# Retention, Fourier mixing and an MLP on one core: the first batch rebuilt (half tables mirrored, loads and units in another order, sums moved into PSUM)

## The chip, the cores and the metric

The kernel runs on one core of one Trainium2 chip. The metric is the device time of one execution in microseconds (us). Before the change it is 247.04 us, the median of three runs (246.52 to 247.95).

## The reference, cut to what matters

```
# q, k, v: (4, 8, 768, 64) f32;  w_ch1: (512, 2048), w_ch2: (2048, 512) f32
gamma = 1 - 2 ** (-5 - arange(8));  scale = 1 / 8
for t in range(768):                                  # per batch and head
    state = gamma * state + outer(k[t], v[t])
    y[t] = scale * q[t] @ state
x = y as (4, 768, 512)
mixed = real(fft(fft(x, axis=1), axis=2))
u = x + mixed
un = (u - mean(u)) / sqrt(var(u) + 1e-6)              # over the last axis
out = u + relu(un @ w_ch1) @ w_ch2
```

## The kernel before

**Stages of a batch.** The batch has 6 chunks of 128 rows and 4 pairs of heads, worked in the order PAIR_ORDER. For each pair q, k and v are loaded as f32 and cast to f16, k scaled by the decay (`kd`); q and k are transposed on TensorE. `am` multiplies them within a chunk (wkA), `ae` masks and scales the result on VectorE (atm). `kv0` makes one k-v product for each of five chunks (wkK), `sc` (L495) runs the decay over them as a scan. `yi` multiplies atm by v, `yx` multiplies q by the scanned states, both into one PSUM tile (wkY); `x0` (L539) scales that into the rows x. Pairs 0 and 1 of the order fill side 0 of x, pair 2 the columns 2 to 129 of side 1, and pair 3 its columns 130 to 257.

**The Fourier step.** The real part of the two transforms is made from sums and differences. `fold_s` (L679) adds and subtracts the two halves of the rows, `fold_d` (L689) the two sides; `s1` (L736) multiplies by the tables csp and ssp over rows, 193 columns wide, and leaves g; `s2` multiplies g by the tables cd16 and sd16 over columns. Only half of the row frequencies are computed; row blocks 3 to 5 use g mirrored (`gr`, L752). `g0_a`, `g0_b`, `g0_c` make the term of column 0 with the table csn. The tables come from a range reduction in three steps on VectorE (`ts_dve`, `td_dve`; L288, L290, L292) and Abs and Sin on ScalarE (`t_act`, `csn_unit`).

**Row blocks 0 to 2 of batch 0.** `px` (L803) puts half of x's sides into PSUM by multiplying with plus and minus half an identity (hid, nhid), s2 adds the transforms there; ScalarE copies half of the result to qn (L861), VectorE combines it with the other half into u in two instructions (L862, L864). `norm_unit` subtracts the mean (`xmean`, `mean`), giving un; `unT_unit` transposes it.

**The MLP.** For batch 0's first 384 rows `h0_unit(kb, g)` (L953) multiplies one block of 128 rows by four blocks of w1: 16 matmuls. Elsewhere `h_unit` (L936) takes 384 rows. Results are evicted with a relu to ht16, by ScalarE for the rows of ACT_ROWS and by VectorE for the others. `ch_unit` (L979) multiplies by w2, a quarter of a row block per part; L983 makes the output of it, and SP stores it. `rstd_unit` takes the variance (L904, L905) and its root.

**The order.** `first_units` is a list of units for batch 0; each one is pinned behind the one before it on every engine. It ends with un of row block 2; the h0 units stand behind it. Everything else is put out by `emit`, which spreads streams of units over the main line (`majors`: h0, ch, h, ch) by due times between 0 and 1 for each batch (DM0, TS0, DA0, LD0 and so on), and up to time 1.0 `behind` holds it behind the last instruction of `first_units` on its engine; order within an engine is then the tile scheduler's, but POOL's is pinned. All loads of batch 0 are issued by SP at the start, in the order q, k, v of pair 0, of pair 1 and so on. The weights are loaded by POOL (`w1_unit`, `w2_unit`, L993 and L1000). The loads of batch 1 wait for the seventh weight transfer and for `lb[0]["mm"]`, the last matmul of the eighth h0. `filler(n)` multiplies zeros n times (L151); there are 40 such matmuls, all ahead of the first h0.

PSUM has five buffers for general use (`ps_g`), two for y (`ps_y`) and one for the fillers; after `first_units` the last three become `ps_pm`.

Of the kernel before, what the change touches and what calls it, by code (L numbers as in the profile page):

```python
# [18 lines left out]
P = 128  # L19
# [10 lines left out]
PAIR_ORDER = [0, 1, 3, 2]  # L30
ON_ACT = {'q': (0, 1, 0), 'kv': (1, 1, 1), 'g': (0, 1, 1), 'gr': (0, 0, 0)}
FB = 1
DM0, DM1 = (0.120, 0.208, 0.265, 0.344), (0.004, 0.137, 0.232, 0.341)
TS0 = (0.249, 0.368, 0.406, 0.410, 0.479, 0.544, 0.680, 0.685)
TS1 = (-0.040, -0.020, 0.048, 0.585)
DA0, DA1 = (0.068, 0.080, 0.173, 0.203, 0.315, 0.321), (0.063, 0.067, 0.063, 0.158, 0.168, 0.189)
LD0, LD1 = (0.172, 0.226), (-0.370, 0.140)
HT0 = (0.655, 0.675, 0.673, 0.628)
NPE = 2
ACT_ROWS = ((2, 5, 6, 7, 8, 9, 10, 14), (0, 3, 6, 7, 9, 10, 11, 12, 14, 15), (2, 4, 5, 6, 7, 8, 10, 14))  # L40
# [3 lines left out]
def kernel(  # L44
# [13 lines left out]
    def pool(name, bufs, **kw):  # L58
# [37 lines left out]
        "p (n w) -> p n w", n=4)  # L96
    pmask = const.tile([P, 4], f32, tag="pmask")
# [82 lines left out]
    for i in range(4):  # L180
        load_unit(0, i)()
# [3 lines left out]
    icol = const.tile([P, 8], f32, tag="icol")  # L185
# [6 lines left out]
    kf_i = tmp[:, 0, 0:KN].bitcast(i32)  # L192
    kf = tmp[:, 1, 0:KN]
    rs = [tmp[:, 2 + n] if n < 4 else tmp2[:, n - 4] for n in range(10)]
# [6 lines left out]
    nc.gpsimd.iota(kf_i, pattern=[[1, KN]], base=0, channel_multiplier=0)  # L201
    nc.gpsimd.memset(wz, 0.0)  # L202
    filler(6)()
    for h in range(H):
# [3 lines left out]
    nc.vector.tensor_scalar(out=gexp[:, 0], in0=lgrow, scalar1=icol[:, 3:4],  # L208
                            scalar2=float(math.log(0.125)), op0=ALU.mult, op1=ALU.add)
    nc.vector.tensor_scalar(out=gexp[:, 1], in0=lgrow, scalar1=icol[:, 5:6], scalar2=None,  # L210
                            op0=ALU.mult)
    nc.scalar.activation(gexp, gexp, AF.Exp, bias=0.0, scale=1.0)
    for h2 in range(2):
        nc.scalar.activation(gk2[D * h2:D * h2 + D], lgrow[D * h2:D * h2 + D, h2:H:2], AF.Exp,
                             bias=0.0, scale=float(P))
    nc.scalar.activation(icol[:, 6:7], lgrow[:, 0:1], AF.Sin, bias=0.0, scale=1.0)
# [6 lines left out]
    nc.vector.tensor_scalar(out=icoln[:, 0:3], in0=icol[:, 0:3],  # L223
                            scalar1=float(np.float32(1.0 / S)), scalar2=None, op0=ALU.mult)
    nc.vector.tensor_scalar(out=icoln[:, 3:5], in0=icol[:, 3:5], scalar1=float(1.0 / DM),
                            scalar2=None, op0=ALU.mult)
    nc.vector.tensor_copy(kf, kf_i)

    def gk_unit(hp):
        def run():  # L230
            nc.scalar.copy(gk5[:, hp, :, 1:], gk2[:, hp:hp + 1].unsqueeze(1).to_broadcast(
                [P, D, NCH - 2]))
        return run
# [7 lines left out]
    def half_tables():  # L241
        nc.vector.tensor_scalar(out=last[:, 0:1], in0=icol[:, 0:1], scalar1=float(P - 1),
                                scalar2=1.0, op0=ALU.is_equal, op1=ALU.mult)
        for n, (m, a) in enumerate(((-0.5, 1.0), (-1.0, 1.0), (-2.0, 0.0))):
# [8 lines left out]
                                scalar2=1.0, op0=ALU.mult, op1=ALU.mult)  # L253
        nc.vector.tensor_scalar(out=t2[:, 3, 0:128], in0=sd16[:, 0, 1:257:2], scalar1=halve,
                                scalar2=1.0, op0=ALU.mult, op1=ALU.mult)
# [11 lines left out]
    m2 = const.tile([P, 1], f32, tag="m2c")  # L267
    odd = const.tile([P, 1], f32, tag="oddc")

    def parity_consts():  # L270
        nc.vector.tensor_scalar(out=m2, in0=icol[:, 0:1], scalar1=0.5, scalar2=-0.25,
                                op0=ALU.mult, op1=ALU.add)
        nc.vector.tensor_scalar(out=m2, in0=m2, scalar1=MAGIC, scalar2=-MAGIC,
                                op0=ALU.add, op1=ALU.add)
        nc.vector.scalar_tensor_tensor(out=odd, in0=m2, scalar=-2.0, in1=icol[:, 0:1],
                                       op0=ALU.mult, op1=ALU.add)
# [3 lines left out]
        nc.vector.tensor_scalar(out=sgn, in0=odd, scalar1=-2.0, scalar2=1.0,  # L280
                                op0=ALU.mult, op1=ALU.add)

    def trig_dve(idx, n, w, col, coln):
        r = rs[2 * idx][:, 0:w]
        ra = rs[2 * idx + 1][:, 0:w]

# [895 lines left out]
```

## Time and profile before

| | us |
|---|---|
| median of three runs | 247.04 |
| span of the profiled execution | 245.4 |
| first h0 matmul (L953) starts | 35.08 |
| TensorE idle from 35 to 90 us | 0.9 |
| VectorE busy from 25 to 30 us | 4.93 of 5.00 |
| last scan (L495) ends | 26.30 |
| first load of batch 1 is issued | 44.89 |

In the profile PE is TensorE's matmuls, PEld its weight loads, DVE VectorE, ACT ScalarE, POOL GpSimd, SP the queue that issues DMAs. A row of the windows has the window, its length, the busy time of each engine with the number of instructions, the granted clock of TensorE, the share of the DMA engines and GB/s. A row of the order of time has start, duration, engine, line, operation and tiles; in square brackets stands how long the engine was idle before it and what ended that.

### The profile page before, as it was taken

How to read it: one execution, taken by the hardware profiler on the slowest of the kernel's cores; microseconds unless marked ns; L12 is line 12 of the kernel's file. 1: busy time of each engine (PE TensorE's matmuls, PEld its weight loads, DVE VectorE, ACT ScalarE, POOL GpSimd, SP SyncE). 2: the span in 40 equal slices, each digit the busy share in tenths (PEclk: the TensorE clock that was granted, in tenths of full speed). 3: DMA queues.
4: the chain of work that ended last, by engine and by line, in shares of the span. 5: the costliest groups of instructions: out<-in, count | busy, mean ns of one | idle time of the engine just before them, and what ended most of it. 6: DMA issues, size and time to landing. Idle time of an engine off the chain costs nothing.

```text
span 245.4 us, 5309 instructions
## 1 busy us (share of the span) xinstructions
PE 234.2 (95%) x2024; PEld 143.8 (59%) x2024; DVE 177.0 (72%) x430; ACT 124.2 (51%) x276; POOL 81.7 (33%) x146
## 2 busy tenths in 40 slices
PE   6997899999999998999999999999999999999995
PEld 2454668956776655665567546655666455445543
DVE  8997957897897788996885748887895656424112
ACT  8798669587775434751247414742247317202500
POOL 6667601465600057690000646660002405000000
PEclk9999999999999999999999999999999999999999
DMA  8999999699999377999999667786200241221012
GB/s 173 256 260 140 204 195 205 164 245 230 291 229 222 75 168 165 191 181 137 256 272 214 116 141 203 129 120 139 87 1 0 45 151 21 47 85 43 0 45 85
DMA packets 99209, 36.39 MB, mean 148 GB/s; under 512 B 89840, under 2 KB 96240, under 8 KB 99184
## 3 DMA queue, kind: packets, MB, share of 16 engines
q1 hardware_dynamic: 94960, 31.86, 62.2%
q0 software_dynamic: 4224, 4.19, 10.7%
q8 instruction: 16, 0.26, 0.5%
q14 instruction: 9, 0.07, 0.1%
HBM read 27.26 MB, written 6.29 MB: 137 GB/s over the span
## 4 chain that ended last, share of the span: by engine, by line
PE 71%; DMA 7%; DVE 7%; POOL 4%; ACT 4%; SPq 3%; issue 1%; POOLq 0%; ACTq 0%; DVEq 0%
PE psc L979 30%; PE psh L936 25%; DMA k<-in_k_dram 5%; PE ps L736 3%; SPq L165 3%; PE wkA L600 3%; DMA q<-in_q_dram 2%; PE wkY L654 2%; PE pq L833 2%; PE wkY L650 1%; POOL u L870 1%; PE wkK L619 1%; ACT un L885 1%; DVE bst L889 1%; POOL kd L407 1%
## 5 line engine op out<-in xcount | busy, mean ns | idle before, releaser
L979 PE MATMUL psc<-w,ht 128*128 128x512 f16 (+2 forms) x400 | 89.3, 371 | 0.0
L936 PE MATMUL psh<-unT,w 128*128 128x384 f16 x448 | 81.6, 326 | 0.4 <-ACT ht L940 0.2
L979 PEld LDWEIGHTS <-ht 128*128 128x128 f16 x400 | 37.5, 98 | 36.5 <-issue 0.2
L936 PEld LDWEIGHTS <-w 128*128 128x128 f16 x448 | 42.3, 98 | 24.7 <-issue 1.4
L940 ACT ACTIVATE ht<-psh 128x384 f16<-128x384 f32 x64 | 30.9, 489 | 41.7 <-PE psh L936 41.1
L870 POOL TENSOR_TENSOR u<-u,x 128x256 f32<-128x256 f32 x21 | 13.3, 635 | 100.3 <-DVE u L840 91.0
L983 DVE SCALAR_TENSOR_TENSOR ob<-psc,stats,u 128x512 f32<-128x512 f32 (+2 forms) x25 | 18.1, 726 | 26.1 <-PE psc L979 26.0
L942 DVE TENSOR_SCALAR ht<-psh 128x384 f16<-128x384 f32 x48 | 26.2, 548 | 7.7 <-PE psh L936 7.4
L603 DVE TENSOR_TENSOR atm<-wkA,maskp 128x512 f16<-128x512 f32 x36 | 23.8, 681 | 1.6 <-PE wkA L600 1.6
L891 ACT ACTIVATE un<-u,stats 128x512 f16<-128x512 f32 x21 | 15.2, 722 | 16.7 <-DVE stats L890 12.1
L889 DVE BATCH_NORM_STATS2 bst<-u 128x6 f32<-128x512 f32 x21 | 14.6, 694 | 7.7 <-POOL u L872 7.6
L629 DVE SCALAR_TENSOR_TENSOR s<-s,gk,wkK 128x128 f16<-128x128 f16 x48 | 16.3, 341 | 3.7 <-ACT s L625 2.7
L662 ACT ACTIVATE x<-wkY,gexp 128x384 f16<-128x384 f32 x24 | 12.8, 581 | 8.0 <-PE wkY L654 8.0
L151 PE MATMUL wps<-ht 128*128 128x512 f16 x40 | 13.5, 444 | 2.2 <-POOL ht L202 2.2
L383 POOL TENSOR_SCALAR kd<-k,gexp 128x384 f16<-128x384 f32 x24 | 13.8, 585 | 3.6 <-DMA k<-in_k_dram 3.6
L872 POOL TENSOR_TENSOR u<-u,x 128x256 f32<-128x256 f32 x21 | 13.3, 635 | 3.0 <-DVE stats L890 3.0
L600 PE MATMUL wkA<-qTz,kT 128*128 128x256 f16 x72 | 13.4, 273 | 0.1
L835 ACT COPY qn<-pq 128x128 f32<-128x128 f32 x18 | 4.9, 272 | 13.6 <-PE pq L833 13.6
L953 PE MATMUL psh<-unT,w 128*128 128x128 f16 x192 | 11.5, 219 | 0.1
L953 PEld LDWEIGHTS <-w 128*128 128x128 f16 x192 | 11.0, 98 | 0.7 <-issue 0.5
L840 DVE SCALAR_TENSOR_TENSOR u<-pq,g,qn 128x256 f32<-128x256 f32 x18 | 8.5, 472 | 3.3 <-PE psh L936 2.5
L388 POOL TENSOR_SCALAR v<-v 128x768 f16<-128x768 f32 x12 | 10.0, 831 | 1.3 <-DMA v<-in_v_dram 1.3
(164 smaller groups left out, 315.6 us busy)
## 6 DMA issues: line engine op xcount, KB each, us to landing
q<-in_q_dram SPq DMA_DIRECT2D x16, 384.0 KB, 6.3
k<-in_k_dram SPq DMA_DIRECT2D x16, 384.0 KB, 5.6
v<-in_v_dram SPq DMA_DIRECT2D x16, 384.0 KB, 6.3
out_dram<-ob SPq DMA_DIRECT2D x23, 256.0 KB, 2.6
w<-in_moe_w_ch_dram POOLq DMA_DIRECT2D x8, 512.0 KB, 10.8
unT<-un SPq DMA_TRANSPOSE x15, 2.4
out_dram<-ob SPq DMA_DIRECT2D x1, 192.0 KB, 1.9
qTz<-q16z SPq DMA_TRANSPOSE x8, 3.9
```

The lines of the kernel that those rows point to most:

```text
L600: mm = nc.tensor.matmul(wk[:, c2], st["kT"][:, c, :], st["qT"][:, :, c, :], start=True, stop=True)
L603: nc.vector.tensor_tensor(out=st["atm"][:, 2 * part:2 * part + 2], in0=wk, in1=maskp[:, PAIR_ORDER[i]].unsqueeze(1).to_broadcast([P, 2, 2, ...
L629: nc.vector.scalar_tensor_tensor(out=s16[:, c], in0=s16[:, c - 1], scalar=gk2[:, hp:hp + 1], in1=wk[:, c - c0], op0=ALU.mult, op1=ALU.add)
L870: nc.gpsimd.tensor_tensor(out=u[:, kb, 0:256], in0=u[:, kb, 0:256], in1=x[:, kb, 0, 1:257], op=ALU.add)
L889: nc.vector.bn_stats(bst, u[:, kb, :])
L891: una = nc.scalar.activation(un, u[:, kb, :], AF.Identity, bias=stats[:, kb, 0:1], scale=-1.0)
L936: nc.tensor.matmul(psh, w116[:, cb, fb * P:(fb + 1) * P], unT[:, cb, rt * 384:(rt + 1) * 384], start=(cb == 0), stop=(cb == 3))
L940: nc.scalar.activation(ht16[:, fb, :], psh, AF.Relu, bias=0.0, scale=-1.0)
L942: nc.vector.tensor_scalar(out=ht16[:, fb, :], in0=psh, scalar1=-1.0, scalar2=0.0, op0=ALU.mult, op1=ALU.max)
L953: mm = nc.tensor.matmul(psh[:, f], w116[:, cb, fb * P:(fb + 1) * P], unT[:, cb, kb * P:(kb + 1) * P], start=(cb == 0), stop=(cb == 3))
L979: nc.tensor.matmul(psc[:, c0:c1], ht16[:, fb, rb3 * P:(rb3 + 1) * P], w216[:, fb, c0:c1], start=(fb == 0), stop=(fb == NFB - 1))
L983: nc.vector.scalar_tensor_tensor(out=ob[:, c0:c1], in0=psc[:, c0:c1], scalar=lb[b]["st"][:, rb, 3:4], in1=lb[b]["u"][:, rb, c0:c1], op0=AL ...
```

## The change

- Batch 0's twelve loads are issued in the order LOADS: q0, k0, q1, k1, v0, q2, v1, k2, q3, k3, v2, v3.
- The range reduction covers 194 and 129 columns instead of 386 and 257. Its steps are single units on a named engine (`trig`). The other halves of the tables are mirrored by `mir_s` and `mir_d` with a sign per partition; csn is copied out of csp. `turn_d` makes tables for the upper columns with the sign turned.
- Casts, copies and evictions of batch 0 take the engine as an argument ("A" ScalarE, "V" VectorE, "P" GpSimd).
- The second half of the columns no longer goes through fold_d. Its S1 product is summed in PSUM from both sides: the part of side 0 early (`s1a_pre`, `s1b_pre`), that of side 1 after the last fold_s (`s1a_fin`, `s1b_fin`). `minus_unit` supplies side 0 with its sign turned.
- Row blocks 0 to 2: px puts x itself into PSUM with the identity, and `s2e_unit` adds both halves of the columns there, eight matmuls per row block instead of four. `un0_unit` takes un straight out of PSUM; u is written later by `u0_unit`. qn, mu and the two combining instructions go away. Row block 0 is split in two PSUM tiles.
- The list `first_units` is in a new order and holds the h0 units, `g0`, csn and `u0` too; in `majors` twelve empty units stand in their place. The PSUM pools are exchanged in the list (`second`).
- The fillers: six at the start and six single ones, 12 in place of 40.
- The due times and ACT_ROWS have other values; the sine half of the tables t2 has its sign turned.

```diff
+LOADS = (('q', 0), ('k', 0), ('q', 1), ('k', 1), ('v', 0), ('q', 2), ('v', 1), ('k', 2), ('q', 3), ('k', 3), ('v', 2), ('v', 3))
+SW, DW = 194, 129
-DM0, DM1 = (0.120, 0.208, 0.265, 0.344), (0.004, 0.137, 0.232, 0.341)
-TS0 = (0.249, 0.368, 0.406, 0.410, 0.479, 0.544, 0.680, 0.685)
+DM0, DM1 = (0.225, 0.285, 0.339, 0.379), (0.019, 0.164, 0.328, 0.362)
+TS0 = (0.237, 0.364, 0.355, 0.47, 0.519, 0.549, 0.621, 0.693)
...
-LD0, LD1 = (0.172, 0.226), (-0.370, 0.140)
+LD0, LD1 = (0.262, 0.373), (-0.339, -0.001)
...
-ACT_ROWS = ((2, 5, 6, 7, 8, 9, 10, 14), (0, 3, 6, 7, 9, 10, 11, 12, 14, 15), (2, 4, 5, 6, 7, 8, 10, 14))
+ACT_ROWS = ((2, 4, 5, 6, 7, 8, 9, 10, 11, 13), (0, 1, 4, 5, 7, 8, 9, 10, 14, 15), (1, 4, 5, 8, 9, 10, 12, 13, 14, 15))
...
-    for i in range(4):
-        load_unit(0, i)()
+    for name, i in LOADS:
+        load0(name, i)
...
+    def trig(idx, part, eng):
+        n, w, c = (S, SW, idx) if idx < 3 else (DM, DW, idx)
+        r, ra = rs[2 * idx][:, 0:w], rs[2 * idx + 1][:, 0:w]
+
+        def run():
+            if part == 0 and eng == "A":
+                nc.scalar.activation(ra, kf[:, 0:w], AF.Copy, bias=MAGIC, scale=icoln[:, c:c + 1])
+            elif part == 0:
+                eng_of(eng).tensor_scalar(out=ra, in0=kf[:, 0:w], scalar1=icoln[:, c:c + 1],
+                                          scalar2=MAGIC, op0=ALU.mult, op1=ALU.add)
+            elif part == 1:
+                eng_of(eng).tensor_scalar(out=ra, in0=ra, scalar1=-MAGIC, scalar2=float(n),
+                                          op0=ALU.add, op1=ALU.mult)
+            else:
+                eng_of(eng).scalar_tensor_tensor(out=r, in0=kf[:, 0:w], scalar=icol[:, c:c + 1],
+                                                 in1=ra, op0=ALU.mult, op1=ALU.subtract)
+        return run
...
+    def mir_s(which, eng):
+        def run():
+            tab = (csp, ssp)[which]
+            dst = bass.AP(tensor=tab.tensor, offset=tab[:, 0, 0, 97:98].offset,
+                          ap=[list(tab.ap[0]), [3 * NK - 1, 2], [NK, 3], [1, 96]])
+            src = bass.AP(tensor=tab.tensor, offset=tab[:, 0, 0, 95:96].offset,
+                          ap=[list(tab.ap[0]), [3 * NK, 2], [NK, 3], [-1, 96]])
+            scaled(eng, dst, src, (sgn, nsgn)[which])
+        return run
...
+    def minus_unit(eng):
+        def run():
+            dst, src = fd[0]["eo"][:, 1, :, :, 128:256], fd[0]["ab"][:, :, :, 0, 130:258]
...
+    def s1_last(part, e, c0, c1, start, pars=(0, 1)):
+        ps, off = (fd[0]["psA"][:, e], 0) if c1 == 64 else (fd[0]["psB", e], c0)
...
+        for par in pars:
+            for sb in range(3):
...
+                nc.tensor.matmul(ps[:, par, c0 - off:c1 - off], lhs, tab[:, par, sb, c0:c1],
+                                 start=start and par == 0 and sb == 0, stop=False,
+                                 skip_group_check=True)
...
+            for n, (dst, rhs) in enumerate(((lo[:, 0:256], x[:, 0, 1:257]),
+                                            (lo[:, 256:257], x[:, 1, 257:258]),
+                                            (up, x[:, 1, 256:1:-1]))):
+                nc.tensor.matmul(dst, ident16, rhs, start=n == 0 or n == 2 and kb in SPLIT,
+                                 stop=False, skip_group_check=True)
...
+    def s2e_unit(kb, cb, halves=(0, 1)):
+        def run():
+            g = fd[0]["g"]
+            for half in halves:
+                for e in range(2):
+                    tab = ((cd16, sd16), (cdr, sdr))[half][e]
+                    nc.tensor.matmul(lb[0]["pq", kb, half], g[:, 2 * e + cb, kb * P:kb * P + P],
+                                     tab[:, cb], start=False, stop=cb == 1 and e == 1,
+                                     skip_group_check=True)
+        return run
...
+            if eng == "A":
+                una = nc.scalar.activation(un, pq, AF.Identity, bias=xm, scale=-1.0)
+            else:
+                una = nc.vector.tensor_scalar(out=un, in0=pq, scalar1=-1.0, scalar2=xm,
+                                              op0=ALU.mult, op1=ALU.add)
...
+            trig(3, 1, "V"), q0_unit(2), ae_unit(0, 1, 0), gk_unit(1), filler(1), kv0_unit(1),
+            ae_unit(1, 0, 1), trig(3, 2, "V"), x_edges(1), t_act(4, 0), ae_unit(0, 0, 0),
+            ae_unit(1, 1, 0), sc_unit(1), t_act(3, 2), yi_unit(0, 0), k0_unit(2, 0, "A"),
...
+            am_unit(3, 1), ae_unit(3, 0, 1), t_act(1, 2), t_act(4, 1), sc_unit(2), t_act(0, 2),
+            v0_unit(3, 0, 3, "A"), yx_unit(2), x0_unit(2, 0, "A"), s1a_pre(0), yi_unit(2, 1),
+            x0_unit(2, 1, "A"), w1_unit(1), ae_unit(3, 0, 0), v0_unit(3, 3, 6, "P"), kv0_unit(3),
+            ae_unit(3, 1, 0), t_act(3, 1), ae_unit(3, 1, 1), yi_unit(3, 1), s1b_pre(0),
+            turn_d(1, "P"), mir_s(1, "A"), yi_unit(3, 0), sc_unit(3), w1_unit(2), w1_unit(3),
+            yx_unit(3), s1b_pre(1), s1a_pre(1), fold_s(0, 0, 130, 1, 2, (0,), "V"),
+            fold_s(0, 0, 130, 1, 2, (1,), "V"), fold_d(0, 0, (0,), "V"), s1_mm(0), parity_b,
+            x0_unit(3, 0, "A"), fold_d(0, 0, (1,), "V"), s1_mm(1), x0_unit(3, 1, "A"),
+            fold_s(0, 130, 258, 1, 2, (0,), "V"), s1a_fin(0),
+            fold_s(0, 130, 258, 1, 2, (1,), "V"), s1b_fin(0), s1a_fin(1), g_unit(0, "V"),
+            mir_d(0, "A"), turn_d(0, "P"), g_unit(1, "A"), s1b_fin(1), px_unit(0),
+            s2e_unit(0, 0, (0,)), ga_unit("V"), xmean_unit(0), gb_unit(0, "V"), gr_unit(1, "V"),
+            s2e_unit(0, 1, (0,)), s2e_unit(0, 0, (1,)), s2e_unit(0, 1, (1,)), gb_unit(1, "V"),
+            px_unit(1), un0_unit(0, 0, "A"), unT0(0, 0), ut0(0, 0, "A"), w2_unit(0),
+            xmean_unit(1), s2e_unit(1, 0, (1,)), s2e_unit(1, 1, (1,)), un0_unit(0, 1, "V"),
+            unT0(0, 1), s2e_unit(1, 0, (0,)), second, s2e_unit(1, 1, (0,)), ut0(0, 1, "V"),
+            h0_unit(0, 0), px_unit(2), s2e_unit(2, 0, (1,)), un0_unit(1, 2, "V"), unT0(1, 2),
...
+            h0_unit(2, 0), csn_unit(0, "V"), h0_unit(2, 2), csn_unit(1, "P"), g0_unit(0, (1,)),
+            g0_unit(0, (2,)), u0_unit(0, 0, "V"), u0_unit(2, 2, "V"), u0_unit(0, 1, "A"),
+            u0_unit(1, 2, "A"),
+        ]
...
         if b == 0:
-            for kb in range(3):
-                if kb:
-                    majors.append(unT_unit(0, kb))
-                majors += [h0_unit(kb, g) for g in range(4)]
+            majors += [lambda: None] * 12
```

## The prediction

> **What bounds the kernel now.** I read the span and the busy shares first, then the busy time by windows, then the order of time up to 50 us, last the waits of TensorE.
>
> ```profile
> span 245.4 us, 5309 instructions
> ...
> PE 234.2 (95%) x2024; PEld 143.8 (59%) x2024; DVE 177.0 (72%) x430; ACT 124.2 (51%) x276; POOL 81.7 (33%) x146
> ```
>
> The page: the span of the profiled execution is 245.4 us, the median of the runs 247.04 us, so 1.6 us lie around the span and are added at the end. The windows show where PE is not full (time, then PE, PEld, DVE, ACT, POOL busy):
>
> ```profile
> 10.00:15.00 5.00, 4.66 (x74) 2.83 (x69) 4.61 (x14) 4.40 (x10) 3.30 (x6) 1.00 1.27 250
> ...
> 25.00:30.00 5.00, 4.29 (x57) 2.75 (x53) 4.93 (x13) 3.39 (x8) 3.37 (x5) 1.00 1.23 203
> 30.00:35.00 5.00, 4.70 (x39) 3.17 (x39) 3.99 (x12) 2.96 (x11) 0.00 (x0) 1.00 1.24 206
> 35.00:40.00 5.00, 4.85 (x75) 4.22 (x74) 2.77 (x10) 4.39 (x16) 0.26 (x4) 1.00 1.18 193
> ...
> 90.00:245.00 155.00, 151.24 (x1108) 88.57 (x1105) 101.69 (x235) 59.87 (x141) 43.23 (x73) 1.00 0.56 117
> ```
>
> From 35 us on PE is full: idle 0.9 us up to 90 us, and 3.8 us after that, of which 2.9 us are the last eviction and store. Ahead of 35 us part of PE's busy time is the 40 fillers (L151), and DVE is the fullest engine with work (4.93 of 5.00 us). So the kernel is a **start of 35 us, set by loads and DVE, and then a queue of PE work**. A change to the first batch is worth: how much earlier the first h0 matmul (L953) starts, minus PE work that it puts behind that point. The order of time shows the start (start, us, engine, line):
>
> ```profile
> 7.70 0.98 POOL L423 TENSOR_SCALAR v<-v 128x768 f16<-128x768 f32 x1 [0.38 <-DMA v<-in_v_dram]
> ...
> 15.34 0.59 POOL L407 TENSOR_SCALAR kd<-k,gexp 128x384 f16<-128x384 f32 x1 [0.82 <-DMA k<-in_k_dram]
> ...
> 17.04 0.94 POOL L423 TENSOR_SCALAR v<-v 128x768 f16<-128x768 f32 x1 [0.55 <-DMA v<-in_v_dram]
> ...
> 25.49 0.81 DVE L495 TENSOR_TENSOR_SCAN s<-gk,wkK 128x320 f16<-128x320 f32 x1
> ...
> 28.74 0.62 DVE L679 TENSOR_TENSOR xab<-x 128x384 f16<-128x384 f16 x2
> 29.39 1.03 DVE L689 TENSOR_TENSOR eo<-xab 128x768 f16<-128x768 f16 x2
> ...
> 35.08 3.00 PE L953 MATMUL psh<-unT,w 128*128 128x128 f16 x48
> ```
>
> A cast that waits for a DMA tells when it lands. Three loads take 4.65 us (v at 7.70, 12.37, 17.04); a q lands 1.2 us after the load before it, a k or v 1.7 to 1.8. The last scan ends at 26.30, the last fold_s at 29.36, h0 starts at 35.08.
>
> **The change, part by part.**
>
> Loads. The same twelve in a new order; by these spacings k3 lands at 18.2 (before: cast at 21.41), v0 at 10.7 (before 7.70), v2 at 19.9, v3 at 21.6 as before. SP issues nothing else until 44.89. The chain behind v is cast, kv0, scan, yx; the chain behind k has transposes, am, ae and yi too, so what lands last has less behind it.
>
> Tables. The trig steps on DVE cost 1.3 + 1.9 + 2.0 us (386 wide: L288, L290, L292) and 0.7 + 1.1 + 2.0 us (257 wide): 9.0 us. Halved in width and with six of fifteen steps on ACT and POOL some 2.5 us stay on DVE. ACT's table functions (L316 to L325, L301: about 10 us) go to some 5 us, and mirroring adds about 2.5 us on ACT and POOL. DVE takes in exchange three of eight te copies (no row; L925, 512 f16 out of PSUM on DVE, is 0.40 us, so 0.6; above that the 0.80 of ACT's L447), one x0 (nearest L942, 0.55) and one half of k0.
>
> DVE then has this to do between the scan of the first pair and the last fold_s: 4 scans at 0.81 (3.2), 14 ae at 0.49 (6.8; L471, 7.9 us for 16), two te (1.2), x0 (0.5), two trig steps of 129 (0.4 to 0.6), fold_s 1.00 + 0.63 + 0.62, fold_d of the first half 1.03, parity_b 0.35, and one wait of 0.3 for yi of pair 1: 16.1 us. The first scan can't start until v0 has landed, 10.7, been cast on POOL, 0.9, and kv0 has run, 0.5: **12.2 us**. So the last fold_s ends at 28.3, against 29.36. The bounds: if te takes 0.80, the trig steps 0.8 us more and ACT (by the same count full to 24 us) is late with x0, 29.4, no gain; if DVE were free, the chain behind v3 alone counts: 21.6 + cast 0.55 + kv 0.47 + scan 0.81 + yx 0.46 + two x0 1.05 + fold_s 0.62 = 25.6. I take 28.3, for DVE has no hole in that stretch for the order to fill.
>
> From the last fold_s to h0. Before: second fold_d, S1, copies, s2, two evictions, un, transposes, copies: 35.08 - 29.36 = 5.7 us. After: fold_d and the qn and u steps leave this path. PE has left: 18 short S1 matmuls at 0.065 (between L953's 0.0625 and L736's 0.087): 1.2; px twice 0.5; twelve s2e matmuls at 0.11 (L849: two in 0.22) 1.8 with their changes of weights, less what overlaps; two half transposes 0.25: 3.8 us with hand-overs of 0.1. Beside it run ga and gb on DVE (0.35 each), g_unit on ACT (0.60), un0 (0.40) and ut0 (0.37): none is later than the PE step that wants it, by 0.3 us for the tightest (un0 of the first half at 30.95, its transpose 31.0). If that cover is gone, each adds its own 0.4. Start of h0: 28.3 + 3.9 = **32.2 us, 2.9 earlier**. Bounds: 29.5 to 35.
>
> PE work put behind that point: px(2) 0.25, eight s2e of row block 2 0.9 (its four s2 matmuls stood ahead of h0 before), g0_b 0.37 (nine at 0.04, before in an idle spot): **+1.5 us**. The 28 fillers less free no time by themselves: they stood in PE's idle time.
>
> Weights. w1(0) is issued on POOL near 19.6 instead of 20.41, w2 near 29 to 31.5 instead of 25.4 to 28.4, both still ahead of the DMA engines (share 1.2 from 25 to 40 us). The loads of batch 1 (before at 44.89) wait for the eighth h0 and w_dma[6], both some 2.5 us earlier: no cost taken; up to 1.5 us if the weights slip.
>
> Behind h0. Retuned due times and ten ACT rows instead of eight, ten and eight: PE's idle time there, about 2 us without the end, is all that can be won; taken as 0, bounds -1.5 and +4 (below).
>
> Sum: -2.9 + 1.5 = -1.4 us on 245.4: 244.0, and with the 1.6 us around it **245.6 us**.
>
> **Rivals.**
>
> *The start shrinks to what the v chain needs* (the order found is better than my count): last fold_s at 25.6 to 26.5, h0 at 29.5 to 30.4: -4.7 to -5.6 + 1.5: 243 to 244. For it: v3 is the only landing after 20 us. Against: DVE's 16 us.
>
> *Debt behind h0: slower.* In the trace the s2 of row blocks 3 to 5, the zeroing of qTz and the eight maskp (ACT, 1.7 us) run under h0, from 38 to 50 us. Now all of batch 0's h0 belong to the pinned list, and behind() keeps everything else behind its last instruction on each engine, at 46.5 us. DVE then has u0 0.95, zeros 1.5, three bn 2.6 (L904, L905), three s2 with bn 5.5 (0.96 + 0.87 each), three ob evictions 2.2: 12.8 us, to 59.5 us; POOL casts batch 1 only behind the u adds, at 56 (before 49.19). PE has s2 1.3 and twelve ch parts 10.3 until 58.1, then needs unT of row block 5, which comes at 59.5 or later, or the casts. Up to 1.4 us of stall some first transposes of batch 1 fill; from 2.6 us on it is slower by over 0.5%. With 4 us: 248.2; and later casts could carry it to 249.
>
> *PE loses its full rate: slower.*
>
> ```profile
> 2.15 2.74 PE L151 MATMUL wps<-ht 128*128 128x512 f16 x6 [2.15 <-POOL ht L202]
> ...
> 7.89 0.81 PE L151 MATMUL wps<-ht 128*128 128x512 f16 x3
> ```
>
> The first six fillers take 0.46 us each, those at 7.89 take 0.27, though the granted clock reads 1.00 in both windows: PE ran at half rate until it had been busy for some 5.5 us. With 12 fillers instead of 40 PE is busy about half the time from 8 to 28 us. If it falls back, the 3.8 us to h0 grow by about 2.5 and the first h0 by up to 1.7: 248 to 250. Against: no PE hole of my count is longer than 1.5 us. The Trainium skill (TensorE: Matmul & The Clock Gate, "Part 1: The HAM clock gate") gives a window of 3.4 us of idleness for the fall and as much activity for the rise; by that rule the rate would hold here, and the trace's rise after 5.5 us is of that order.
>
> *It changes nothing*: new waits between queues that are worked in order eat the 2.9 us: 246.5 to 247.5.
>
> **How the numbers follow.** 0.5% (1.2 us) is about what a measurement of this kernel can tell from no change. Chances: my sum 0.48 (its own range 244.4 to 246.8, two thirds of it below 245.8), v chain 0.23, debt 0.14, half rate 0.08, nothing 0.07. Faster: 0.32 + 0.23 = 0.55. Slower: 0.12 of the debt's, 0.08: 0.20. Same: the rest, 0.25. Low end: between the v chain's times, less 1 us for idle time won behind h0, 242.3; high end 249.0, in the half rate's span.
>
> **What would show it.** First L953 matmul near 32.2; last scan near 25.7 with DVE over 95% busy from 12 to 28 us; v3's cast at 21.7 or later and not the last wait; no PE hole over 0.5 us between 28 and 46; h0 done near 46, s2 of block 3 only after that. Wrong if DVE has holes ahead of the scans (then loads or POOL casts set the start), if 128-column matmuls take 0.1 us after 28 us, or if PE idles over 1 us between 55 and 62.

## The result and the profile after

The changed kernel takes **251.27 us** (median of 4 runs, 251.03 to 251.92) against 247.02 us (4 runs, 246.52 to 247.95): a ratio of 1.0174, 95% interval 1.0150 to 1.0198. It is slower by 4.3 us, where 1.4 us faster was forecast, and it lies above the forecast's high end of 249.0. In the changed kernel the lines are: L155 filler, L483 transposes, L492 te, L509 am, L516 ae, L531 kv0, L540 scan, L559 yi, L571 yx, L724 fold_s, L947 s2e, L1126 h0. In runs that add a line to the kernel they are one higher (L541 scan, L1127 h0).

The page of the kernel after: the span, the engines, and the granted clock in 40 slices.

```profile
span 249.0 us, 5322 instructions
...
PE 234.2 (94%) x2041; PEld 146.8 (59%) x2041; DVE 174.2 (70%) x415; ACT 123.7 (50%) x278; POOL 81.0 (33%) x148
...
PEclk9759799999999999999999999999999999999999
```

PE's busy time is the same 234.2 us as before, in a span that is 3.6 us longer. Ahead of h0 it is 28.9 us before and 26.8 after, with 28 fillers fewer; behind h0 it is 2.2 us more. The clock row, full before, has holes in the first 30 us. The windows of the kernel after:

```profile
10.00:15.00 5.00, 3.91 (x42) 2.39 (x41) 4.05 (x11) 4.35 (x11) 2.71 (x5) 0.50 1.25 257
15.00:20.00 5.00, 4.58 (x60) 3.16 (x59) 4.28 (x8) 2.88 (x6) 2.32 (x6) 0.59 1.30 243
20.00:25.00 5.00, 3.39 (x59) 2.09 (x57) 4.77 (x9) 3.46 (x7) 4.26 (x7) 1.00 0.43 60
25.00:30.00 5.00, 4.43 (x76) 3.64 (x74) 4.29 (x11) 3.82 (x11) 1.88 (x3) 0.66 1.14 181
...
60.00:65.00 5.00, 3.77 (x41) 2.71 (x41) 4.42 (x15) 4.91 (x8) 5.00 (x8) 1.00 1.12 262
65.00:80.00 15.00, 14.48 (x184) 10.33 (x182) 13.56 (x36) 12.50 (x26) 4.53 (x7) 1.00 0.91 188
```

DVE is not full between 10 and 30 us (4.05 to 4.77 of 5.00), the DMA engines fall to a share of 0.43 from 20 to 25 us, and behind h0 PE has a hole of 1.23 us at 60 to 65 and 0.52 at 65 to 80. The order of time on DVE, ahead of h0, shows the waits (start, duration, then in brackets the idle time and what ended it):

```profile
13.03 0.82 DVE L540 TENSOR_TENSOR_SCAN s<-gk,wkK 128x320 f16<-128x320 f32 x1 [0.91 <-PE wkK L531]
...
18.36 0.96 DVE L492 COPY qTz<-tq 128x768 f16<-128x768 f16 x1 [0.37 <-PE tq L483]
...
22.15 0.95 DVE L492 COPY qTz<-tq 128x768 f16<-128x768 f16 x1
23.02 1.31 DVE L724 TENSOR_TENSOR xab<-x 128x774 f16<-128x774 f16 x2
...
28.04 0.82 DVE L540 TENSOR_TENSOR_SCAN s<-gk,wkK 128x320 f16<-128x320 f32 x1 [0.68 <-PE wkK L531]
...
30.98 0.63 DVE L724 TENSOR_TENSOR xab<-x 128x384 f16<-128x384 f16 x2 [0.39 <-ACT x L337]
```

The last fold_s ends at 31.61, not 28.3, and the row of all h0 matmuls puts the first at 35.1, where it was before:

```profile
L1126 PE MATMUL psh<-unT,w x192: 218/219/219, 35.1 to 47.3; 128*128 128x128 f16 x192
```

POOL's order of time shows two things: `mir_s(0)` holds up the queue for 2.8 us until ACT has made csp, with POOL's half of k3's cast and w1's first transfer behind it; and behind h0 the u adds begin at 53.73 (42.44 before), so that the casts of batch 1 begin at 58.59 (49.19 before).

```profile
20.66 0.75 POOL L339 TENSOR_SCALAR csp<-csp,sgn 128x576 f16<-128x576 f16 x1 [2.81 <-ACT csp L325]
21.38 0.58 POOL L453 TENSOR_SCALAR kd<-k,gexp 128x384 f16<-128x384 f32 x1
21.91 0.96 POOL L1167 DMA_DIRECT2D w<-in_moe_w_ch_dram  x1
...
53.73 0.64 POOL L1055 TENSOR_TENSOR u<-u,x 128x256 f32<-128x256 f32 x1 [17.70 <-DVE stats L1081]
...
58.59 0.83 POOL L415 TENSOR_SCALAR q16z<-q 128x768 f16<-128x768 f32 x1
```

The account of the two profiled executions, then: start of h0 35.1 in both; from there to the end 210.3 us before and 213.9 after. PE's busy time in that stretch is 205.3 us in 1699 matmuls before and 207.5 in 1721 after (+2.2), its idle time 5.0 and 6.4 (+1.4).

### The profile page after: what moved, and what is told of

The parts are those of the page before. It is cut to its first block, busy times and chain, and to the rows that moved or that the text cites. A ratio compares the mean times of both kernels' runs of the same rounds, so it can differ in the third digit from the quotient of the medians.

```text
span 249.0 us, 5322 instructions
## 1 busy us (share of the span) xinstructions
PE 234.2 (94%) x2041; PEld 146.8 (59%) x2041; DVE 174.2 (70%) x415; ACT 123.7 (50%) x278; POOL 81.0 (33%) x148
## 4 chain that ended last, share of the span: by engine, by line
PE 74%; DVE 7%; DMA 6%; ACT 5%; POOL 4%; SPq 2%; issue 2%; ACTq 0%; DVEq 0%
PE psc L1153 29%; PE psh L1109 22%; PE psh L1126 4%; DMA unT<-un 3%; PE ps L856 2%; PE wkA L645 2%; DMA k<-in_k_dram 2%; DVE atm L516 2%; PE wkY L699 2%; PE wkY L695 1%; DMA v<-in_v_dram 1%; ACT kT L612 1%; POOL u L1057 1%; PE pq L1027 1%; ACT un L1070 1%
## 5 line engine op out<-in xcount | busy, mean ns | idle before, releaser
L1153 PE MATMUL psc<-w,ht 128*128 128x512 f16 (+2 forms) x400 | 88.3, 370 | 0.0
L1113 ACT ACTIVATE ht<-psh 128x384 f16<-128x384 f32 x70 | 34.0, 490 | 46.9 <-PE psh L1109 46.5
L1115 DVE TENSOR_SCALAR ht<-psh 128x384 f16<-128x384 f32 x42 | 22.9, 551 | 9.9 <-PE psh L1109 9.5
L1070 ACT ACTIVATE un<-u,stats 128x512 f16<-128x512 f32 x21 | 15.2, 722 | 15.8 <-DVE stats L1069 10.6
L1126 PE MATMUL psh<-unT,w 128*128 128x128 f16 x192 | 11.4, 219 | 0.0
L1126 PEld LDWEIGHTS <-w 128*128 128x128 f16 x192 | 11.0, 98 | 0.1
L645 PEld LDWEIGHTS <-kT 128*128 128x128 f16 x72 | 6.8, 98 | 4.6
L724 DVE TENSOR_TENSOR xab<-x 128x780 f16<-128x780 f16 (+4 forms) x18 | 8.8, 526 | 0.8 <-ACT x L337 0.4
```

The costliest lines, as they stand in the source:

```text
L645: mm = nc.tensor.matmul(wk[:, c2], st["kT"][:, c, :], st["qT"][:, :, c, :], start=True, stop=True)
L1070: nc.scalar.activation(un, u[:, kb, :], AF.Identity, bias=stats[:, kb, 0:1], scale=-1.0)
L1113: nc.scalar.activation(ht16[:, fb, :], psh, AF.Relu, bias=0.0, scale=-1.0)
L1115: nc.vector.tensor_scalar(out=ht16[:, fb, :], in0=psh, scalar1=-1.0, scalar2=0.0, op0=ALU.mult, op1=ALU.max)
L1126: mm = nc.tensor.matmul(psh[:, f], w116[:, cb, fb * P:(fb + 1) * P], unT[:, cb, kb * P:(kb + 1) * P], start=(cb == 0), stop=(cb == 3))
L1153: nc.tensor.matmul(psc[:, c0:c1], ht16[:, fb, rb3 * P:(rb3 + 1) * P], w216[:, fb, c0:c1], start=(fb == 0), stop=(fb == NFB - 1))
```

## The experiments

"H0" is the start of the first h0 matmul, "scan to h0" the time from the start of the first scan to it. The first scan lies between 12.5 and 13.4 us in kernels whose lists agree up to there, so H0 carries some scatter that scan to h0 leaves out. In five profiles whose list up to h0 is that of the kernel after, H0 is 34.9 to 35.4, and in a sixth, d1_s2e, 36.2: one profile each doesn't carry a difference of some tenths. Times are medians of 4 runs (f3_late 10, h4_mend 6); ratios are to the kernel before, run beside each, whose median lay between 246.5 and 247.2. Differences in time below are taken from the ratios. The intervals of e1_warm, e2_pool, e4_fence, e9_norm and d1_s2e overlap that of the kernel after, so their times alone don't tell them from it.

| run | edit | time | ratio, 95% | H0 | scan to h0 |
|---|---|---|---|---|---|
| before | | 247.02 | 1 | 35.1 | 23.3 |
| after | | 251.27 | 1.0150-1.0198 | 35.1 | 22.1 |
| f1_few | before, 12 fillers | 249.36 | 1.0075-1.0131 | 37.3 | 25.6 |
| e1_warm | after, 40 fillers | 250.41 | 1.0110-1.0166 | 34.0 | 21.1 |
| e2_pool | after, mir_s(0) late | 250.78 | 1.0133-1.0189 | 34.4 | 21.3 |
| d2_te | after, te copies cut | 249.72 | 1.0086-1.0132 | 34.0 | 20.9 |
| e3_te | after, te on ACT | 254.12 | 1.0244-1.0318 | 36.8 | 24.0 |
| l1_loads | after, old loads | 252.43 | 1.0197-1.0241 | 36.8 | 22.6 |
| h1_three | e1, e2, d2 | 249.33 | 1.0056-1.0122 | 34.1 | 20.7 |
| d1_s2e | after, s2e doubled | 252.52 | 1.0188-1.0248 | 36.2 | 23.1 |
| e4_fence | after, early fence | 250.53 | 1.0133-1.0176 | 34.9 | 22.2 |
| e5_due | after, old due times | 253.05 | 1.0226-1.0286 | 34.9 | 22.1 |
| e6_rows | after, old ACT rows | 253.76 | 1.0252-1.0298 | 35.4 | 22.8 |
| e9_norm | after, sums under h0 | 250.96 | 1.0139-1.0221 | 35.0 | 22.1 |
| h2_best | e1, e2, e9 | 249.56 | 1.0059-1.0115 | 33.5 | 21.0 |
| h4_mend | h2 and more | 251.46 | 1.0153-1.0213 | 36.5 | 23.1 |
| f2_rows | before, new ACT rows | 249.74 | 1.0080-1.0114 | 34.8 | 23.1 |
| f3_late | before, new later batches | 247.77 | 1.0007-1.0036 | 35.1 | 23.3 |

### The start

**Fillers.** e1_warm puts 28 fillers into nine lines of the new list, so that it has 40, as many as the kernel before; its recorded expectation counts 22 and 34. f1_few takes 28 out of the old list, the same number that the change takes out. One line of each edit, e1_warm's first:

```diff
-            filler(1), icoln_unit, te_unit(0, 1, "V"), am_unit(0, 0), trig(3, 0, "A"),
+            filler(3), icoln_unit, te_unit(0, 1, "V"), am_unit(0, 0), filler(6), trig(3, 0, "A"),
...
-              q0_unit(0), t0_unit(0, 0), filler(4), ts_dve(1), te_unit(0, 0), t_act(0, 2),
+              q0_unit(0), t0_unit(0, 0), filler(1), ts_dve(1), te_unit(0, 0), t_act(0, 2),
```

> The changed kernel with 22 more filler matmuls in the gaps of the first batch (34 of the 40 of before). Theory clock: TensorE at half rate from 9 to 20 us and from 27 to 30 us is what ate the 2.9 us expected of the start; at full rate its steps there are shorter, the first h0 matmul moves from 35.09 to 33 to 34, the time falls by 1 to 2 us. Rival theory, queues: VectorE's list and waits on casts set the start, the rate hardly matters; h0 at 34.7 to 35.5, time within 0.5 us. In both the granted clock reads 1.00 from 10 us on.

> The kernel before with 12 filler matmuls instead of 40, nothing else. Theory clock: without them TensorE falls to half rate here too, somewhere between 8 and 30 us; h0 starts at 35.6 to 36.6 instead of 35.08 and the time is up 0.5 to 1.5 us. Rival (the old order keeps TensorE busy enough, or its rate does not matter where VectorE is full): rate 1.00 or h0 within 0.3 us, time within 0.4 us; fillers out of the way could even win 0.3.

With 40 fillers PE keeps its rate (the clock reads 1.00, and six wkY matmuls take 0.35 us and the ten of kv0 0.47 all along) and H0 comes 1.1 us earlier. The time falls by 0.9 us. In the old list the cut alone costs 2.5 us. The same six S1 matmuls in f1_few, and in the kernel before, in the order of time on PE:

```profile
28.70 1.15 PE L736 MATMUL ps<-csp,eo 128*128 128x193 f16 x6 [0.55 <-DVE eo L689]
```

```profile
28.41 0.69 PE L736 MATMUL ps<-csp,eo 128*128 128x193 f16 x6 [0.41 <-DVE eo L689]
```

They take 1.15 instead of 0.69 us: PE has lost its full rate on the very path to h0, with no hole longer than 1.25 us on PE ahead of it. In f1_few the last fold_s ends at 29.65 (29.36 before) and h0 begins 7.7 us later instead of 5.7, so nearly all of its loss lies in that chain.

**One instruction in POOL's queue.** e2_pool moves mir_s(0) behind v3's cast.

```diff
-            mir_s(0, "P"), ae_unit(2, 1, 1), filler(1), te_unit(3, 0, "V"),
+            ae_unit(2, 1, 1), filler(1), te_unit(3, 0, "V"),
...
-... v0_unit(3, 3, 6, "P"), kv0_unit(3),
+... v0_unit(3, 3, 6, "P"), mir_s(0, "P"), kv0_unit(3),
```

> The changed kernel with mir_s(0) moved on GpSimd from ahead of k0(3) to behind the cast of v3; it stood 2.8 us waiting for ScalarE's table and held up k0(3), the issue of w1(0) and the cast of v2. Theory queues (head of the line): k0(3) at 18.5 to 19.5 instead of 21.38, w1(0) issued by 20.2 instead of 21.91, loads of batch 1 at 43.5 to 44.5 instead of 45.63, h0 0.3 to 1 us earlier, time down 0.3 to 1 us. Theory VectorE's work alone: weights and loads earlier as said, h0 within 0.2 us, time within 0.3 us.

w1's first transfer is issued at 18.95 instead of 21.91, POOL's half of k3 is cast at 18.42 instead of 21.38, the DMA share from 20 to 25 us is 1.09 instead of 0.43, and H0 comes 0.7 us earlier. That the edit did this is not shown. Up to the third scan nothing on DVE moved, and the gain lies behind it, where PE in this execution kept its rate. DVE in the kernel after, then DVE and the window of 25 to 30 us in e2_pool:

```profile
25.18 0.80 DVE L540 TENSOR_TENSOR_SCAN s<-gk,wkK 128x320 f16<-128x320 f32 x1
```

```profile
25.20 0.80 DVE L540 TENSOR_TENSOR_SCAN s<-gk,wkK 128x320 f16<-128x320 f32 x1
...
27.48 0.82 DVE L540 TENSOR_TENSOR_SCAN s<-gk,wkK 128x320 f16<-128x320 f32 x1
```

```profile
25.00:30.00 5.00, 4.31 (x89) 3.48 (x88) 4.86 (x12) 4.61 (x13) 2.90 (x4) 1.00 0.61 87
```

The last scan waits for nothing here; in the kernel after it waited 0.68 us for a kv0 of 0.74 us, which takes 0.47 in e2_pool. PE does the same work at the same times up to 26.5 us in both, and then the same kind of six psA matmuls takes 0.50 us in the one and 0.35 in the other. Whether the edit or chance kept the rate, one profile can't tell, and the times don't differ.

**VectorE's share of the copies.** d2_te leaves most of the q copies of te out of VectorE; e3_te gives them back to ScalarE.

```diff
-                    "p (t c) -> p t c", c=NCH), tq.rearrange("p c t -> p t c"))
+                    "p (t c) -> p t c", c=NCH)[:, 0:n], tq.rearrange("p c t -> p t c")[:, 0:n])
...
-            te_unit(2, 0, "V"), t_act(1, 0), q0_unit(3), mir_d(1, "P"), t_act(1, 1),
+            te_unit(2, 0, "A"), t_act(1, 0), q0_unit(3), mir_d(1, "P"), t_act(1, 1),
```

> The changed kernel, but the copies of the q table that stand on VectorE take only 16 of the 128 columns of each chunk, so part of the mixed-in table is left out. It takes 0.95 us to some 0.2 from each of the two copies in DVE's list ahead of the last fold. The theory that DVE's list is full there: the last fold_s ends 1.0 to 1.5 us earlier (31.6 in the changed kernel) and h0 starts at 33.6 to 34.1 (35.1). The rival, that waits for ScalarE's and PE's products set the scans and DVE's work fits into them: less than 0.4 us of it arrives at h0, and the time stays within 0.5 us.

> The changed kernel with the two strided q copies te(2,0) and te(3,0), 0.96 and 0.95 us on VectorE, given back to ScalarE. Theory VectorE's work: its list from the first scan to the last fold_s is 1.9 us shorter, last fold_s ends near 30 instead of 31.6, h0 at 33.3 to 33.8, time down 1.2 to 1.8 us. Theory queues (waits for other engines set the start, ScalarE is as full): h0 at 34.5 to 35.5, time within 0.6 us.

d2_te: 1.4 us less on DVE, H0 1.1 us earlier, 1.6 us faster: the list counts. e3_te, which moves te(3, 0) as well, missed: scan to h0 grew by 1.9 us, with 4.6 us of waits in ae and the scans. But in its profile PE stood at half rate until about 31 us, so that six wkY matmuls took 0.50 us as late as 29.84:

```profile
29.84 0.50 PE L559 MATMUL wkY<-v,atm 128*128 128x64 f16 x6
```

The same half rate goes with 1.0 us more from scan to h0 in d1_s2e below. So about half of the loss can be ScalarE's, and this run doesn't divide it. All four runs of e3_te (252.75 to 254.79 us) are slower than those of the kernel after, so ScalarE was no better place for the copies.

**Loads.**

> The changed kernel with the loads of the kernel before in their order: q, k and v of one pair together, where the change puts the four v behind. By my sum v2 and v3 last free the k and q tables of the last pairs 1.7 to 1.9 us earlier, at the price of v0 coming later: k3's cast moves from 21.4 to about 23, the last scan from 28.0 to 29.5 or later, and h0 from 35.1 to 36 to 37. The rival, that the last scan waits for compute and not for a load: h0 within 0.5 us of 35.1, and then the new order of loads brought nothing.

`LOADS` as before, q, k, v by pairs: H0 36.8, 1.7 us later, and 1.1 us slower. Of the 1.7 us, 1.2 stand at the first scan already (14.21 instead of 13.03), where the order of loads was to act; the rest comes in an execution whose clock stayed low for longer (0.72 from 30 to 35 us instead of 1.00).

**All three at once.**

> The changed kernel with three things at once: 22 more fillers, mir_s(0) behind v3's cast on GpSimd, and the two q table copies of VectorE's list cut to 16 of 128 columns (part of the mixed-in table is left out). One by one they brought h0 forward by 1.06, 0.74 and 1.09 us from 35.09. If they are separate causes (rate, waits, VectorE's work) they add up: last fold_s near 28.7, h0 at 32.0 to 32.6, which is where my forecast put it, and a time 2.5 to 3 us under the changed kernel's, 248.3 to 248.8. The rival is one common limit that each of them eased: h0 not before 33.4 and a time over 249.3.

They don't add up: H0 34.1, scan to h0 shorter by 1.4 us, not by the 3.0 of the three runs together. Divided at the third scan:

| run | first to third scan | third scan to h0 |
|---|---|---|
| after | 12.15 | 9.91 |
| e1_warm | 11.29 | 9.82 |
| e2_pool | 12.05 | 9.15 |
| d2_te | 11.01 | 9.89 |
| h1_three | 10.90 | 9.83 |

e1_warm and d2_te gain ahead of the third scan, and their gains overlap there; e2_pool's gain, behind it, is gone in h1_three. DVE's order of time in h1_three:

```profile
24.26 0.82 DVE L541 TENSOR_TENSOR_SCAN s<-gk,wkK 128x320 f16<-128x320 f32 x1 [0.60 <-PE wkK L532]
...
27.21 0.82 DVE L541 TENSOR_TENSOR_SCAN s<-gk,wkK 128x320 f16<-128x320 f32 x1 [0.76 <-PE wkK L532]
```

The scans wait for kv0, and kv0 stands on PE behind a transposition's copy on ScalarE (0.89 us of wait in am) and behind three fillers (0.8 us each time). With less work DVE only waits more, for PE, ACT and DVE hand each pair round. PE and DVE are some 85% busy between the first scan and the last fold_s here, and ACT 76%.

### Behind h0

**The work put there.** d1_s2e issues the eight s2e matmuls of row block 2 twice; all eight units stand behind the first h0 in the list, not six of them as its expectation says.

> The changed kernel with the eight s2e matmuls of row block 2 (six of the eight stand behind the start of h0, all of them in PE's full stretch) issued twice, so that row block 2 gets its transform twice. My forecast put 0.9 us on them as part of 1.5 us of PE work that h0's move leaves behind its start, counted in full. If that is right, the time grows by 0.8 to 1.0 us, to 252.1 to 252.3, and h0 stays at 35.1 within 0.5. The rival, that the work behind h0 hides in PE's later waits (1.8 us of them between 50 and 80 us): less than 0.4 us.

The time grows by 1.1 us, its interval touches that of the kernel after (1.0188 against 1.0198), and H0 moved too, by 1.1, in a list that is the same up to h0. The order of time of its PE shows why (first row), beside that of the kernel after (second):

```profile
19.88 0.50 PE L559 MATMUL wkY<-v,atm 128*128 128x64 f16 x6 [0.42 <-DVE atm L516]
```

```profile
19.84 0.35 PE L559 MATMUL wkY<-v,atm 128*128 128x64 f16 x6 [0.42 <-DVE atm L516]
```

In this execution PE stood at half rate until 31.4 us, though its clock column reads 1.00. From h0 to the end it has 0.5 us more than the kernel after, PE busy 0.7 more. So the work put behind h0 costs between nothing and about its own time; one for one is not shown.

**The cover.** e4_fence lets everything else start behind the exchange of the PSUM pools instead of behind the whole list; e9_norm puts the sums, the three s2 and their norms among the h0 units. e7_under and e8_all did the same without moving the norms back: DVE's bn then stood in its queue waiting for POOL's u, h0 itself waited 2.5 and 3.4 us for an eviction, and the times were 253.98 and 254.17; they say nothing of the debt.

```diff
-    base.update(tails)
+        if u is second:
+            base.update(tails)
...
+            u0_unit(2, 2, "V"), h0_unit(0, 1), unT0(2, 2), ut0(2, 2, "A"), s2_unit(0, 3),
+            h0_unit(1, 3), s2_unit(0, 4), h0_unit(1, 1), norm_unit(0, 3), h0_unit(0, 3),
+            s2_unit(0, 5), norm_unit(0, 4), h0_unit(2, 3), unT_unit(0, 3), h0_unit(2, 1),
+            h0_unit(2, 0), unT_unit(0, 4), h0_unit(2, 2), norm_unit(0, 5),
```

> The changed kernel with the fence (the instructions that hold everything else behind the first batch) taken ahead of the first h0 instead of behind the last unit. By the instruction order the zeroing of qTz, the half tables and maskp then run under h0; s2 of row blocks 3 to 5 still comes behind h0. Theory debt: 1.5 us of zeros and 1.7 us of maskp less ahead of s2; u adds at 52 instead of 53.73, casts of batch 1 at 56.5 to 57 instead of 58.59, TensorE idle from 55 to 80 us 0.3 to 1.0 instead of 1.75, time down 0.5 to 1.3 us. Rival (the PSUM tiles held until u0, or the loads, set it): idle and time within 0.4 us.

> The changed kernel with h0's cover used for the rest of batch 0: its sums csn, g0, gr and u0, the last three s2 chunks and the norms of mix 0 stand among the h0 units instead of behind them, and each norm stands two h0 units behind its s2, so that DVE isn't held at a bn that waits for POOL's u. The debt theory (VectorE and GpSimd come out of h0 some 9 us behind, and PE pays for it between 50 and 80 us): the batch-1 casts start at 48.5 to 50 (58.6 in the changed kernel), PE's idle from 50 to 80 is under 0.5 us, and the time is 1.2 to 2 us under the changed kernel's, 249.3 to 250. The rival (the idle behind h0 is a matter of the order of ScalarE's and PE's lists, not of the debt): the idle from 50 to 80 stays above 1.2 us and the time within 0.5 us of the changed kernel's. An h0 that itself waits for DVE (an ht eviction over 1 us late) would make it no test.

e4_fence: u adds at 51.50, casts at 56.35; 0.5 us faster by the ratios, within their intervals, of which H0 explains 0.2. PE's waits moved from 60 to 50-60 us, and from 55 to 80 us it is idle for 1.5 us where 0.3 to 1.0 was expected. e9_norm paid the debt, casts at 49.62, and won nothing (250.96). Its POOL, and its PE, by the order of time:

```profile
49.62 0.83 POOL L415 TENSOR_SCALAR q16z<-q 128x768 f16<-128x768 f32 x1 [0.18 <-PE psh L1127]
```

```profile
47.41 0.40 PE L1097 MATMUL pst<-ident,un 128*128 128x128 f16 x4 [1.10 <-ACT un L1071]
...
50.20 0.40 PE L1097 MATMUL pst<-ident,un 128*128 128x128 f16 x4 [0.61 <-ACT un L1071]
```

The idle time from 50 to 80 us fell from 1.77 to 0.82, and 1.51 us appeared between 45 and 50, where PE waits for un in the two rows above. We read this as the chain s2, u, bn, un, transpose waited for at another place; its length was not measured.

**Due times and rows.**

> The changed kernel with the due times DM0, TS0 and LD0 of before; the fence behind the last unit of the first batch stays. Theory debt: what starves TensorE from 60 to 65 us (1.2 us idle) is that GpSimd's u adds and then the casts of batch 1 come late, because the variance of row blocks 0 to 2 stands ahead of s2 on VectorE; with s2 first the u adds start near 51.5 instead of 53.73, the casts near 56 instead of 58.59, the idle time from 60 to 80 us falls from 1.7 to under 0.6 us, time down 0.8 to 1.7 us. Rival, late loads: the loads of batch 1 (45.63) set it; idle time and time within 0.4 us.

> The changed kernel with the rows of the table that ScalarE evicts in the later batches as they were before. They act only behind batch 0, so h0 stays at 35.1 within 0.3. My forecast put nothing on them: the time within 0.5 us of the changed kernel's. The rival, that the new split is part of the 3.6 us by which the stretch behind h0 is longer: 1 us or more faster, with PE's idle from 90 us on under 4 us (4.68 in the changed kernel, 3.76 before).

> The kernel before with the change's ten ACT rows in each place instead of eight, ten and eight, and nothing else. In the changed kernel the old rows cost 2.5 us. If the new rows are better by themselves (VectorE relieved where it holds up PE), the kernel before gets 0.5 to 2.5 us faster, and then the first batch of the change costs more than the whole change shows. The rival, that the rows only fit the new due times: 247.0 or slower.

> The kernel before with the change's ACT rows and its due times for the later batches (the second values of DM, DA and LD, and TS1); batch 0 is the old one throughout. If the later batches of the change are better by themselves, it is 0.5 to 3 us faster than the kernel before and PE's idle from 90 us on falls below 3.3 us (3.76). The rival, that these values are neutral and fitted to the new first batch: within 0.6 us of 247.0, or slower.

Each old value in the new kernel costs 2.0 (due times of batch 0) or 2.5 us (rows), and the new rows alone in the old kernel cost 2.4. e5_due brought the u adds to 51.54 as expected, but the casts only to 57.70 and PE's idle time from 60 to 80 us from 1.75 to 1.18; from h0 to the end PE had 1.0 us more busy and 0.65 more idle time. So each value suits the list that it was set for; that the rows are better by themselves was wrong. All new values for the later batches in the old kernel give 247.77, 1.0007 to 1.0036: its stretch behind h0 is 211.2 us instead of 210.3, with PE's work the same (205.4) and 0.8 us more idle. The values gain nothing.

### Everything mended

> The changed kernel, complete, with 22 more fillers, mir_s(0) behind v3's cast on GpSimd, and batch 0's sums, s2 chunks and norms among the h0 units. From the single runs h0 should start 1.8 us earlier, at 33.3, and the stretch from h0 to the end, 213.4 to 213.9 us in all of them, should stay: a span of 246.8 to 247.2 and a time of 248.8 to 249.4, still above the kernel before (247.0). The rival, that an early start is eaten up behind h0 (the stretch grows to 215 us), gives 250.5 or more.

> The changed kernel, complete, with what the runs named: 34 fillers with those ahead of kv0 put behind it, mir_s(0) behind v3's cast, the v casts of pairs 2 and 3 on GpSimd alone and kv0(2) ahead of am(3,0), the sums, s2 and norms of batch 0 among the h0 units, and the transposes of row blocks 3 and 4 one and more h0 units later. If the waits named are the loss, the last scan starts near 25.8, h0 near 32.7, PE's idle from 35 to 80 us falls from 2.3 (h2_best) to under 1.2, the stretch from h0 to the end to 212, the span to 244.7 and the time to 247.0 to 247.8, that of the kernel before. The rival, that each cure opens the next wait: h0 not before 33.3 or the stretch still 213, and a time of 248.6 or more.

h2_best did what was expected: H0 33.5, span 246.8, and a stretch behind h0 of 213.3 us, as in the others. Its 249.56 us is the best of the complete new kernels, and still above the kernel before. h4_mend put the casts of v and kv0 earlier and the fillers behind kv0 as well. DVE had its last scan with no wait ahead of it, but it missed: PE lost its rate at 27 us in spite of 39 fillers, five of which then stand at half rate ahead of yi and yx of the last pair, whose x came late. Its PE (order of time) and the waits of its DVE:

```profile
28.43 0.53 PE L559 MATMUL wkY<-v,atm 128*128 128x64 f16 x6
```

```profile
DVE xab L724 <- ACT x L337: 2.2, 1, 2.2
```

Even its two fastest runs of six, 249.97 and 250.12, are above h2_best's median. No version here beats the kernel before.

## Why the prediction was wrong

**Start of h0, -2.9 us: failed, came out at 0.** The step that failed is the sum for the last fold_s, with its words "DVE has no hole in that stretch". The missing 3.3 us (31.61 instead of 28.3) are, by DVE's order of time:

- The first scan at 13.03 instead of 12.2, 0.8 us. v0's cast ended at 11.45, as summed; but kv0 stands on PE behind the transposes of pair 1, which took 0.85 us at half rate, and began at 12.18. It took 0.74 where the row gave 0.47, and the scan waited 0.91 for it.

```profile
10.62 0.83 POOL L465 TENSOR_SCALAR v<-v 128x768 f16<-128x768 f32 x1 [0.17 <-DMA v<-in_v_dram]
```

```profile
11.11 0.85 PE L483 MATMUL tq<-ident,kd 128*128 128x128 f16 x6
...
12.18 0.74 PE L531 MATMUL wkK<-v,kd 128*64 128x64 f16 x10 [0.22 <-DVE atm L516]
```

- Idle time in the list 1.9 us instead of 0.3: 0.37, 0.45, 0.68, 0.39. The forecast added up DVE's work and let the products of PE and ACT come in time. e1_warm shows one source of the waits, PE's rate, and h1_three another, PE's own order. DVE was 84% busy from 12 to 28 us, not over 95%. Both signs of being wrong came, DVE's holes ahead of the scans, for PE's products and not for loads or POOL's casts, and over 1 us of idle PE, at 60 to 65 us instead of 55 to 62.
- Work 16.7 us instead of 15.8. Two te copies took 0.96 and 0.95; the row taken was a smaller contiguous copy scaled up to 0.6, the bound 0.80 was ScalarE's. Two trig steps took 1.04 instead of 0.4 to 0.6, the first fold_s 1.31 instead of 1.00; a part of it is regained where one instruction starts before the last one's record ends.

From the last fold_s to h0 the forecast of 3.9 us came out as 3.5, partly by luck: sixteen s2e matmuls stand ahead of h0, not twelve, and they took 1.8 us at 0.11 each, so the number was too low and the price too high.

**Half rate, given 0.08: the mechanism came, at another place.** "No PE hole longer than 1.5 us" was right and the conclusion wrong: the rate fell with holes of 0.2 to 1.4 us. Its first fall, between 7.8 and 10.3 us (six wkA matmuls 0.34, then 0.50), comes where PE is busy 2.3 of the 5 us from 5 to 10, against 4.6 to 4.8 in the kernel before, e1_warm and h2_best, which kept it. No threshold follows: the second fall, at 26.5 us, came behind 3.4 busy of 5 us, and e2_pool kept its rate behind 3.5, while h4_mend lost it behind 3.6. In the new list most of the cost came ahead of the 3.8 us chain, not in it; in f1_few it came in the chain, as the rival had it. Fillers are worth 0.9 us in the new list (e1_warm) and 2.5 in the old one (f1_few). That "the 28 fillers less free no time" was true, but the sum put the loss of them at nothing, and they cost. The Trainium skill (TensorE: Matmul & The Clock Gate, "What's actually happening") puts the fall after an idle window of about 3.4 us; the traces here differ, with falls at holes under 1.5 us, and they decide. The same page of the Trainium skill ("A second HAM failure mode: psum-queue depth-cycling") tells of a matmul unit whose rate swings when it is idle often and briefly, which is what these rows look like.

**POOL's queue.** w1(0) "near 19.6" came at 21.91. mir_s was costed as work (2.5 us on ACT and POOL), not as a wait for t_act on ACT, 2.8 us, with k3, w1 and v2 queued behind it. The wait is shown; a cost of it at h0 is not. k3's other half, cast on ACT, came no earlier in e2_pool (21.37 instead of 21.26), and PE began k3's transposes at 22.11 instead of 22.02.

**Loads: right in direction.** l1_loads: 1.2 us at the first scan, 1.7 at h0, part of it PE's rate.

**PE work behind h0, +1.5: about right.** 22 matmuls more; +2.2 us busy in the kernel after, +1.2 in e9_norm and h2_best with the same 22, so 1.5 lies within what such records resolve.

**Idle behind h0, 0: was +1.4.** 1.4 us at 50 to 80 us, 0.5 at 150 to 200, less 0.2 at 80 to 100 and 0.3 at 35 to 45. The rival of the debt described the place, DVE and POOL late, casts at 56 (58.6) and PE idle above 1 us. But its price is not the debt's: paid early (e9_norm) it gave nothing back. What sets it is not shown. The rows of e9_norm point at the chain from s2 to unT; f3_late shows that 0.8 us of such idle time come with the new values for the later batches even in the old kernel. Whether they are the same 0.8 in the new one is not settled.

**Sum.** 0.0 + 2.2 + 1.4 = +3.6 us of span, as measured. The 28 fillers and VectorE's copies are shown as causes of the late start, each by the run that takes it away; together with e2_pool's edit they shorten scan to h0 by 1.4 us, not by the 3.0 of the three single runs. What h1_three still lacks lies in part in kv0's place on PE, behind fillers that keep the rate; h4_mend, which moved it, lost the rate and had x late on ACT. Whether some order of the same list reaches 32.2 stays open.

## What to carry to other kernels

A list of one engine's work is a lower bound for when its last item ends; count for each item also when its operand comes. Here DVE idled for 1.9 of 18.6 us beside a PE that was busy for 15.1 of them. Matmuls that multiply zeros can be worth their place: cutting 28 of them cost the old list 2.5 us, though the same fillers, put ahead of a product that is waited for, held it up by 0.8 us. So such a cut is a change of its own, to be priced alone. For an item moved to an engine worked in order, look up what it waits for at the queue's head (2.8 us here) and whether anything behind it stands on the path; here nothing up to the third scan moved when the wait was taken away. And before a gain or a loss is credited to an edit, compare the time of one small shape in both traces: PE's rate differed between executions by itself.

## What the runs showed of the hardware

The granted clock in the records is no proof of the rate: it read 1.00 in d1_s2e and e3_te through the start while six wkY matmuls took 0.50 us instead of 0.35. A small shape whose time is known is the better meter. Nor is the rate fixed by PE's list alone: the kernel after and e2_pool have the same matmuls at the same times (within 0.1 us) up to 26.5 us, and then 0.50 against 0.35 for six of one shape.

VectorE slowed beside GpSimd. The same trig step on DVE, in the kernel after beside a cast on POOL (13.56 to 14.39), and in h2_best with POOL idle until 13.72:

```profile
13.77 0.70 DVE L306 TENSOR_SCALAR tmp<-tmp 128x129 f32<-128x129 f32 x1
```

```profile
13.22 0.20 DVE L306 TENSOR_SCALAR tmp<-tmp 128x129 f32<-128x129 f32 x1
```

The first fold_s behaves alike: 1.02 us in h1_three with POOL idle beside it, 1.31 in the kernel after and 1.52 in h4_mend, where POOL casts v at the same time. The Trainium skill (GPSIMD Engine Reference, "1. Specifications") says that the two engines share their interface to SBUF, with contention for VectorE instructions of two inputs or in a two-port mode. The fold_s has two inputs, and its rows agree, with 0.3 and 0.5 us for the pair. Whether the trig step, of one input, runs in such a mode no run here shows; it lost 0.5 us.
